# A gather moved behind the bonus products, the first batch's rows turned later, half of the diagonals on ScalarE, and the last rows written in two parts

## The chip, the cores and the metric

The kernel runs on one core of one Trainium2 chip. The metric is the device time of one execution in microseconds (us); lower is better. The profile is one execution taken by the hardware profiler. Its times count from the start of the span. Engines are named as in the profile: PE is TensorE's matmul side and PEld its weight load, DVE is VectorE, ACT is ScalarE, POOL is GpSimd, SP is the engine that issues most DMAs.

## The reference

There are two stages. The first is a linear recurrence with a decaying state for 4 batches, 8 heads, 768 steps and a head dimension of 48:

```python
for t in range(S):
    cur = np.einsum('bhd,bhe->bhde', u[None] * kt, vt)
    y[:, :, t] = np.einsum('bhd,bhde->bhe', rt, state + cur)
    state = w[None, :, :, None] * state + np.einsum('bhd,bhe->bhde', kt, vt)
```

The term with u is the bonus: at its own step a token sees its own k and v weighted by u. The result is laid out as x of 4 batches, 768 tokens and 384 columns. The second stage picks, in each batch, the 128 tokens with the highest score, and only those pass through an MLP:

```python
scores = np.einsum('bsd,d->bs', x, w_gate)
out = x.copy()
for b in range(B):
    top_idx = np.argpartition(-scores[b], capacity)[:capacity]     # capacity = 128
    xe = x[b, top_idx]
    h = np.maximum(xe @ w1, 0.0)                                   # 384 -> 1024
    ye = h @ w2                                                    # 1024 -> 384
    g = 1.0 / (1.0 + np.exp(-scores[b, top_idx]))
    out[b, top_idx] = x[b, top_idx] + g[:, None] * ye
```

## The kernel before

The sequence is cut into units of 128 tokens, six in each batch, 24 in all (NU = 24, NC = 6). Each unit is worked as two halves of 64 tokens. Iteration n of the main loop does a part of unit n - 1, of unit n, of unit n + 1 and of unit n + 2 on different engines. The program order given here is the order in which each engine takes its instructions.

The names: kw is k scaled by powers of the decay; kh and rh are k and r turned by PE and scaled; rp holds the within-unit scores and the state products in PSUM; rk = r * k, rku = rk * u, and du is the sum of rku over each head, the bonus of a token. The matrix at holds du on its diagonal and gets the scores below the diagonal by a masked copy. g and z are states, scr is the product x * w_gate whose sum is the score of a token.

```python
def bonus(n):
    rk = RK[n] = work.tile([128, H, D], F32, name="rk")
    nc.gpsimd.tensor_mul(rk, rpads[n % NIN][:, :, :D], KIN[n])            # line 243
    if n and not picking(n - 1):
        bonus_scaled(n, nc.gpsimd)                                        # rku, line 253

def picking(n):
    return n % NC == 3 and n > NC                                         # n = 9, 15, 21

def diagonal(n):
    AT[n] = work.tile([128, H, C], F32, name="at", bufs=3)
    nc.gpsimd.tensor_mul(AT[n], dia[:, None, :].to_broadcast([128, H, C]),            # line 261
                         DU[n].rearrange("t i p -> t (i p)")[:, :, None].to_broadcast([128, H, C]))
...
for n in range(NU):
    if n == 2:
        late_tables()                  # five small iotas on POOL, lines 222 to 229
    ...
    if n:
        behind = states(n - 1)         # PE line 347, then a mark on ACT (line 351)
    work_at(n, "states")
    products(n)                        # PE line 304
    scores(n)                          # PE line 313
    work_at(n, "scores")
    if picking(n):
        bonus_scaled(n + 1, nc.gpsimd)
    load(n + 4, 0, added(n, 0))        # DVE g, line 328; releases a load of k
    op = masked(n)                     # DVE masked copy, line 318
    load(n + 4, 2, op)
    if n:
        values(n - 1, behind)          # PE line 363, waits for the mark
        finish(n - 1)                  # ACT copies y to x, lines 380 and 382
    if n + 1 < NU:
        pr = turn(n + 1)               # PE lines 270 and 275, ACT kh (line 280)
    if n:
        stored(n - 1)                  # x to DRAM
    if c < NC - 1:
        added(n, 1)                    # DVE g, then ACT z, line 335
    if n + 1 < NU:
        load(n + 4, 1, turned(n + 1, pr))      # DVE rh, line 285
        load(n + 4, 3, bonus_sum(n + 1))       # DVE du, line 257
    if n + 2 < NU:
        scaled(n + 2)                  # POOL kw, line 239
    if n + 1 < NU:
        diagonal(n + 1)                # POOL at, line 261
    if n + 2 < NU:
        bonus(n + 2)                   # POOL rk and rku
    if n:
        weights(n - NC, score(n - 1))  # DVE scr, line 397
    work_at(n, "turn")                 # scores turned along (407, 409), compares (417, 419), ranks, matches (459)
    if n + 1 < NU:
        work_at(n, "end")              # parts of the MLP
```

The second stage is spread over later iterations by a plan. `pick` finds the row numbers idx of the chosen tokens with matmuls (467) and two DVE sums (471, 474). `fetch` gathers these rows from the output in DRAM by an indirect DMA that POOL issues (483). `chosen` turns the rows on PE (499) into xt (ACT, 501). `hidden` and `expert` are the MLP's matmuls (510 and 519), 8 parts each, and `leave` writes the rows back by an indirect DMA (527 and 529):

```python
MOVE0 = (0, 0, 0, 0, 0, 0, 1, 1, 2, 2, 3, 3, 4, 4, 5, 5)
MOVE = (0, 0, 0, 0, 1, 1, 2, 2, 3, 3, 3, 4, 4, 4, 5, 5)

def plan(b):
    n = (b + 1) * NC
    ...
    for z in range(NST):                       # NST = 1
        step(n + 2, "turn", match, b, z)
        step(n + 3, "scores", pick, b, z)
        step(n + 3, "scores", fetch, b, z)
        if b:
            step(n + 5, "scores", chosen, b, z)
        else:
            step(n + 4, "end", chosen, b, z)
    parts = [p for z in range(NST) for p in mlp(b, z)]
    for i, (f, a) in enumerate(parts):
        if b or i >= 2 * NST:
            step(n + 5 + (MOVE if b else MOVE0)[i * 16 // len(parts)], "end", f, *a)
        else:
            step(n + 5, "states", f, *a)
```

After the loop the last batch's tokens are picked, fetched, turned, and their MLP runs alone.

Of the kernel before, what the change touches and what calls it, by code (L numbers as in the profile page):

```python
# [17 lines left out]
def kernel(  # L18
# [23 lines left out]
    nc = tc.nc  # L42
    B, H, S, D = r.shape
    C, T = 64, 128
    NC = S // T
# [16 lines left out]
    work = ctx.enter_context(tc.tile_pool(name="work", bufs=2))  # L62
# [155 lines left out]
    found = const.tile([128, NC], F32)  # L218
    tok = const.tile([128, NU, 5], BF16)

    def late_tables():
        nc.gpsimd.iota(slots, pattern=[[-1, 128]], base=0, channel_multiplier=0,
                       allow_small_or_imprecise_dtypes=True)
        for x in counts:
            nc.gpsimd.iota(x[:, :, 2], pattern=[[-128, NC]], base=-128, channel_multiplier=0,
                           allow_small_or_imprecise_dtypes=True)
        nc.gpsimd.iota(tok[:, :, 0], pattern=[[0, NU]], base=0, channel_multiplier=1,
                       allow_small_or_imprecise_dtypes=True)
        nc.gpsimd.iota(tok[:, :, 1], pattern=[[T, NU]], base=0, channel_multiplier=0,
                       allow_small_or_imprecise_dtypes=True)  # L230
# [10 lines left out]
    def bonus(n):  # L241
        rk = RK[n] = work.tile([128, H, D], F32, name="rk")
        nc.gpsimd.tensor_mul(rk, rpads[n % NIN][:, :, :D], KIN[n])  # L243
        if n and not picking(n - 1):
            bonus_scaled(n, nc.gpsimd)

    def picking(n):

        return n % NC == 3 and n > NC

    def bonus_scaled(n, engine):
        RKU[n] = work.tile([128, H, D], F32, name="rku")
        engine.tensor_mul(RKU[n], RK[n], ub)  # L253
# [4 lines left out]

    def diagonal(n):
        AT[n] = work.tile([128, H, C], F32, name="at", bufs=3)  # L260
        nc.gpsimd.tensor_mul(AT[n], dia[:, None, :].to_broadcast([128, H, C]),  # L261
                             DU[n].rearrange("t i p -> t (i p)")[:, :, None].to_broadcast([128, H, C]))

    def turn(n, keys=None, between=None):
        def two_heads(x, hp):
# [249 lines left out]
    def expert(b, z, f):  # L515
# [5 lines left out]
        if f + 1 == FB:  # L521
            leave(b, z)

    def leave(b, z):
# [4 lines left out]
        st = nc.gpsimd.indirect_dma_start(  # L529
            out=out_rows[: (b + 1) * S, :], out_offset=bass.IndirectOffsetOnAxis(ap=IDX[b, z][:m, :1], axis=0),  # L530
            in_=ot[:m, :], in_offset=None)
# [15 lines left out]
    def step(n, where, f, *a):  # L547
        fill.setdefault((n, where), []).append((f, a))
# [4 lines left out]
        for f in range(FB):  # L553
            yield expert, (b, z, f)


    MOVE0 = (0, 0, 0, 0, 0, 0, 1, 1, 2, 2, 3, 3, 4, 4, 5, 5)
    MOVE = (0, 0, 0, 0, 1, 1, 2, 2, 3, 3, 3, 4, 4, 4, 5, 5)

    def plan(b):  # L560
        n = (b + 1) * NC
        for j in range(NC):
            step(n - NC + j + 2, "turn", scores_along, b, j)
            step(n - NC + j + 2, "turn", compare, b, j)
        step(n + 1, "turn", count, b)
        step(n + 1, "turn", parts_of_scores, b)
        step(n + 2, "turn", rank, b)
        for z in range(NST):
            step(n + 2, "turn", match, b, z)
            step(n + 3, "scores", pick, b, z)  # L570
            step(n + 3, "scores", fetch, b, z)
            if b:
                step(n + 5, "scores", chosen, b, z)
            else:
                step(n + 4, "end", chosen, b, z)
        parts = [p for z in range(NST) for p in mlp(b, z)]
        for i, (f, a) in enumerate(parts):
            if b or i >= 2 * NST:
                step(n + 5 + (MOVE if b else MOVE0)[i * 16 // len(parts)], "end", f, *a)
            else:  # L580
                step(n + 5, "states", f, *a)

    for b in range(B):
        plan(b)
# [1 line left out]
    def work_at(n, where):  # L586
        for f, a in fill.get((n, where), []):
            f(*a)

    bonus(0)  # L590
    warm(10)
    pr = turn(0, k0, key_table)
# [16 lines left out]
    diagonal(0)  # L609
    bonus(1)  # L610
    for n in range(NU):
        if n == 2:
            late_tables()
        b, c = divmod(n, NC)
        if c == 0:
            ZA[n] = zt
        if n:
            behind = states(n - 1)
        work_at(n, "states")
        products(n)  # L620
        scores(n)
        work_at(n, "scores")
        if picking(n):
            bonus_scaled(n + 1, nc.gpsimd)
        load(n + 4, 0, added(n, 0))
        op = masked(n)
        load(n + 4, 2, op)
        if n:
            values(n - 1, behind)
            finish(n - 1)  # L630
        if n + 1 < NU:
            pr = turn(n + 1)
# [50 lines left out]
    for z in range(NST):  # L683
        pick(last, z)
        fetch(last, z)
    some(len(before) - NST)
    for z in range(NST):
        chosen(last, z)
    some(len(before))
    for f, a in after:  # L690
        f(*a)


# [31 lines left out]
```

## Time and profile before

| | before |
|---|---|
| time, median of 3 runs | 164.96 us (164.87 to 165.03) |
| span of the profiled execution | 162.3 us |
| busy PE / PEld | 144.5 / 118.0 us |
| busy DVE / ACT / POOL | 119.6 / 75.9 / 115.2 us |
| mean granted TensorE clock | 0.979 |
| DMA: bytes, mean rate | 24.51 MB, 151 GB/s |
| diagonal (line 261), 24 of them | 28.8 us on POOL, mean 1.20 us |
| score product scr (line 397), 24 of them | 26.3 us on DVE, 0.54 to 4.12 us each |

A line of a timeline has the start, the duration, the engine, the line of the kernel, the operation, the tile written and the tiles read with their shapes, and how many there were; in square brackets stands the idle time before it and what ended that. A line of a table of stretches has the stretch, its length, and then the busy time of PE, PEld, DVE, ACT and POOL with the number of instructions, the granted clock as a share of full speed, the mean busy share of the DMA engines and the rate in GB/s. The chain that ended last is followed back from the last instruction and printed in order of time, with start, duration, engine, tile and line.

### The profile page before, as it was taken

Reading aid. Unit: us, or ns where it says so; the run is one execution under the profiler, and the core shown is the slowest. Engines: PE = TensorE matmul, PEld = TensorE weight load, DVE = VectorE, ACT = ScalarE, POOL = GpSimd, SP = SyncE. Lnnn points to the kernel's source line nnn. Section 1 sums busy time; section 2 is a strip of 40 time slices with the busy share of each in tenths; the row PEclk is TensorE's granted clock in tenths of the full one; section 3 lists DMA queues with packets and bytes.
Section 4 is the critical chain, followed back from the end, with each engine's and each line's share of the span. In section 5 each row is a group of like instructions: output and inputs, shape, how many; then the busy total and the mean of one; then the engine's idle time right before and its main releaser. Section 6 shows DMA issues by size and latency. Waiting matters only on the chain.

```text
span 162.3 us, 8049 instructions
## 1 busy us (share of the span) xinstructions
PE 144.5 (89%) x3374; PEld 118.0 (73%) x3374; DVE 119.6 (74%) x353; ACT 75.9 (47%) x251; POOL 115.2 (71%) x155
## 2 busy tenths in 40 slices
PE   6989978779889948999999999999999999999970
PEld 2577767668777727999786769999877788758730
DVE  7886768889999693358789899999988996701010
ACT  6656565446663631327643747166526565102100
POOL 7389999999999979174798987959999551022002
PEclk9999999999999985799999999999999999999999
DMA  4998999798999986988159989878813104011001
GB/s 74 200 183 155 197 222 208 165 196 188 215 211 223 273 228 163 233 189 220 55 117 253 251 183 206 191 176 181 178 53 101 53 9 146 0 48 49 3 0 48
DMA packets 82660, 24.51 MB, mean 151 GB/s; under 512 B 76352, under 2 KB 82240, under 8 KB 82624
## 3 DMA queue, kind: packets, MB, share of 16 engines
q1 hardware_dynamic: 79888, 19.67, 57.2%
q10 hardware_dynamic: 2224, 2.75, 4.8%
q0 software_dynamic: 512, 1.57, 2.7%
q8 instruction: 27, 0.44, 1.1%
q14 instruction: 9, 0.07, 0.2%
HBM read 18.48 MB, written 5.51 MB: 148 GB/s over the span
## 4 chain that ended last, share of the span: by engine, by line
PE 51%; DVE 18%; issue 11%; POOL 10%; DMA 3%; SPq 2%; ACT 1%; POOLq 1%; DVEq 0%; ACTq 0%
PE m L510 11%; PE rp L304 6%; PE m L519 6%; PE m L270 5%; PE y L347 5%; DVE scr L397 5%; PE rp L313 5%; PE y L363 5%; PE m L275 4%; POOL kw L239 3%; DMA kin<-in_k_dram 2%; DVE oh L459 2%; POOL at L261 2%; DVE at L318 2%; DVE rh L285 2%
## 5 line engine op out<-in xcount | busy, mean ns | idle before, releaser
L261 POOL TENSOR_TENSOR at<-dia,du 128x512 f32<-128x512 f32 x24 | 28.8, 1201 | 14.0 <-DVE du L257 12.6
L397 DVE SCALAR_TENSOR_TENSOR scr<-x,wg 128x384 f32<-128x384 f32 x24 | 26.3, 1094 | 0.4 <-ACT x L382 0.4
L510 PE MATMUL m<-xt,w 128*128 128x128 f32 x192 | 24.6, 286 | 1.7 <-ACT xt L501 1.7
L510 PEld LDWEIGHTS m<-xt,w 128*128 128x128 f32 x192 | 23.5, 201 | 2.4 <-ACT xt L501 2.3
L253 POOL TENSOR_TENSOR rku<-rk,ub 128x384 f32<-128x384 f32 x23 | 23.9, 1040 | 1.6
L239 POOL TENSOR_TENSOR kw<-kin,wk 128x384 f32<-128x384 f32 x23 | 23.3, 1015 | 1.6 <-DMA kin<-in_k_dram 1.6
L335 ACT ACTIVATE z<-g,wp 128x48 f32<-128x48 f32 x80 | 20.2, 325 | 8.6 <-DVE g L328 6.6
L243 POOL TENSOR_TENSOR rk<-rpad,kin 128x384 f32<-128x384 f32 x23 | 23.0, 1001 | 0.0
L380 ACT COPY x<-y 128x192 f32<-128x192 f32 x24 | 7.6, 319 | 32.6 <-PE y L363 30.4
L519 PE MATMUL m<-w,ht 128*128 128x384 f32 x64 | 22.7, 490 | 0.1
L318 DVE COPY_PREDICATED at<-mask,rp 128x512 f32<-128x512 uint32 x24 | 17.6, 732 | 2.7 <-POOL at L261 2.7
L304 PE MATMUL rp<-vpad,kw 128*48 128x96 f32 x288 | 16.7, 257 | 3.0 <-DMA out_dram<-x 1.1
L347 PE MATMUL y<-g,rh 48*64 48x48 f32 x384 | 17.3, 223 | 2.2 <-issue 2.1
L285 DVE TENSOR_TENSOR rh<-m,tables 112x512 f32<-112x512 f32 x24 | 16.4, 683 | 3.0 <-PE m L275 1.6
L347 PEld LDWEIGHTS y<-z,rh 48*64 48x64 f32 x320 | 12.2, 134 | 6.4 <-issue 3.7
L313 PE MATMUL rp<-rh,kh 48*64 48x64 f32 x768 | 16.8, 226 | 0.0
L304 PEld LDWEIGHTS rp<-vpad,kw 128*48 128x48 f32 x288 | 12.7, 127 | 5.2 <-issue 2.3
L419 DVE TENSOR_SCALAR_CACHE_REDUCE gt<-along,sc 128x128 bf16<-128x128 f32 (+5 forms) x24 | 16.2, 675 | 0.0
L257 DVE TENSOR_REDUCE du<-rku 128x8 f32<-128x384 f32 x24 | 13.1, 547 | 3.7 <-POOL rku L253 3.7
L347 PE MATMUL y<-z,rh 48*64 48x48 f32 x320 | 15.4, 223 | 0.5 <-issue 0.5
L270 PE MATMUL m<-ident,kw 128*112 128x128 f32 x92 | 15.0, 285 | 1.0 <-POOL kw L239 0.9
L347 PEld LDWEIGHTS y<-g,rh 48*64 48x64 f32 x384 | 13.8, 134 | 2.8 <-issue 2.6
(99 smaller groups left out, 255.5 us busy)
## 6 DMA issues: line engine op xcount, KB each, us to landing
rpad<-in_r_dram SPq DMA_DIRECT2D x24, 192.0 KB, 4.2
vpad<-in_v_dram SPq DMA_DIRECT2D x48, 96.0 KB, 4.2
kin<-in_k_dram SPq DMA_DIRECT2D x23, 192.0 KB, 4.2
w<-in_moe_w_dram SPq DMA_DIRECT2D x8, 384.0 KB, 4.4
out_dram<-x ACTq DMA_DIRECT2D x14, 192.0 KB, 3.4
out_dram<-x SPq DMA_DIRECT2D x10, 192.0 KB, 3.5
k<-in_k_dram SPq DMA_DIRECT2D x1, 192.0 KB, 2.8
ub<-in_u_dram SPq DMA_DIRECT2D x1, 192.0 KB, 4.3
```

What stands on the lines that cost most here:

```text
L239: (engine or nc.gpsimd).tensor_mul(kws[n % 3][:, :, :D], KIN[n], wk)
L243: nc.gpsimd.tensor_mul(rk, rpads[n % NIN][:, :, :D], KIN[n])
L253: engine.tensor_mul(RKU[n], RK[n], ub)
L261: nc.gpsimd.tensor_mul(AT[n], dia[:, None, :].to_broadcast([128, H, C]), DU[n].rearrange("t i p -> t (i p)")[:, :, None].to_broadcast([128 ...
L270: nc.tensor.transpose(pk[:CH, hp, :], two_heads(kws[n % 3] if keys is None else keys, hp), ident)
L304: nc.tensor.matmul(out=rp[to, hp // 2, at : at + 2 * D], lhsT=kws[n % 3][:, h, :D], rhs=VIN[n][:, h, :], start=True, stop=True)
L313: nc.tensor.matmul(out=rp[ts, i, hp * C : (hp + 1) * C], lhsT=KH[n][rows, hp, ts], rhs=RH[n][rows, hp, ts], start=True, stop=True)
L318: return nc.vector.copy_predicated(at, causal, rp[:, :, : NP * C].rearrange("s i (p t) -> s i p t", p=NP))
L347: mm = nc.tensor.matmul(out=YP[n][i][j * C : (j + 1) * C, hp * D : (hp + 1) * D], lhsT=RH[n][rows, hp, c * C : (c + 1) * C], rhs=z[rows, h ...
L397: return nc.vector.scalar_tensor_tensor(scr, xa[b][:, c, :], 1.0, wg, op0=OP.mult, op1=OP.mult, accum_out=sc[b][:, c : c + 1])
L510: nc.tensor.matmul(out=ph[:, f % 4, :], lhsT=w1[:, d, f * 128 : (f + 1) * 128], rhs=XT[b, z][:, d, :], start=(d == 0), stop=(d == KD - 1))
L519: nc.tensor.matmul(out=pe[:, :Dm], lhsT=HT[b, z][:, f, :], rhs=w2[:, f, :], start=(f == 0), stop=(f == FB - 1))
```

## The change

It has five parts.

- The fetch is issued behind both bonus products on POOL: `pick` and `fetch` move from the place "scores" to a new place "values" (behind the values and before the turning), and rku is always made right behind rk.
- The first batch's rows are turned two iterations after their fetch, as those of the other batches, and its MLP follows the same spread as theirs (MOVE0 goes).
- The iotas move from iteration 2 to the first loads, ahead of the first bonus product.
- In iterations 1 to 10 half of the diagonals (4 of 8 heads) are made by ScalarE as copies with a scale, behind the mark.
- The last batch's second matmul is done in two column halves of 192, each with its own product and its own indirect store of half rows.

The purpose is to take work off POOL where POOL is full, to keep what DVE needs from standing behind the fetch, to keep PE from waiting for the first batch's rows, and to let a half of the last rows leave while PE still works on the other half.

```diff
-    def late_tables():
+    def whole_numbers():
...
         nc.gpsimd.tensor_mul(rk, rpads[n % NIN][:, :, :D], KIN[n])
-        if n and not picking(n - 1):
+        if n:
             bonus_scaled(n, nc.gpsimd)
...
+        du = DU[n].rearrange("t i p -> t (i p)")
+        own = shared(n)
+        nc.gpsimd.tensor_mul(AT[n][:, own:, :], dia[:, None, :].to_broadcast([128, H - own, C]),
+                             du[:, own:, None].to_broadcast([128, H - own, C]))
+
+    def shared(n):
+        return H // 2 if 0 < n < 2 * NC - 1 else 0
+
+    def diagonal_shared(n):
+        du = DU[n].rearrange("t i p -> t (i p)")
+        for h in range(shared(n)):
+            nc.scalar.activation(AT[n][:, h, :], dia, AF.Copy, scale=du[:, h : h + 1])
...
+    def leave_half(b, z, d):
+        m, at = min(128, cap - z * 128), slice(d * Dm // 2, (d + 1) * Dm // 2)
+        ot = work.tile([128, Dm // 2], F32, name="oh", bufs=2 * NST)
+        nc.vector.scalar_tensor_tensor(ot, PE[b, z][:, at], GA[b, z], XR[b, z][:, at], op0=OP.mult, op1=OP.add)
+        nc.gpsimd.memset(spacer, 0.0)
+        st = nc.gpsimd.indirect_dma_start(
+            out=out.rearrange("b s (t d) -> (b s t) d", t=2)[: 2 * (b + 1) * S, :],
+            out_offset=bass.IndirectOffsetOnAxis(ap=HALF[b, z, d][:m, :1], axis=0), in_=ot[:m, :], in_offset=None)
...
-    MOVE0 = (0, 0, 0, 0, 0, 0, 1, 1, 2, 2, 3, 3, 4, 4, 5, 5)
     MOVE = (0, 0, 0, 0, 1, 1, 2, 2, 3, 3, 3, 4, 4, 4, 5, 5)
...
-            step(n + 3, "scores", pick, b, z)
-            step(n + 3, "scores", fetch, b, z)
-            if b:
-                step(n + 5, "scores", chosen, b, z)
-            else:
-                step(n + 4, "end", chosen, b, z)
+            step(n + 3, "values", pick, b, z)
+            step(n + 3, "values", fetch, b, z)
+            step(n + 5, "scores", chosen, b, z)
...
-            if b or i >= 2 * NST:
-                step(n + 5 + (MOVE if b else MOVE0)[i * 16 // len(parts)], "end", f, *a)
-            else:
-                step(n + 5, "states", f, *a)
+            step(n + 5 + MOVE[i * 16 // len(parts)], "end", f, *a)
...
+    whole_numbers()
     bonus(0)
...
-        if n == 2:
-            late_tables()
...
             behind = states(n - 1)
-        work_at(n, "states")
+            diagonal_shared(n)
         products(n)
         scores(n)
         work_at(n, "scores")
-        if picking(n):
-            bonus_scaled(n + 1, nc.gpsimd)
...
             values(n - 1, behind)
             finish(n - 1)
+        work_at(n, "values")
         if n + 1 < NU:
             pr = turn(n + 1)
...
+    for z in range(NST):
+        for d in range(2):
+            at = slice(d * Dm // 2, (d + 1) * Dm // 2)
+            pe = PE[last, z] = psum.tile([128, 512], F32, name="m", bufs=4)
+            for f in range(FB):
+                nc.tensor.matmul(out=pe[:, at], lhsT=HT[last, z][:, f, :], rhs=w2[:, f, at],
+                                 start=(f == 0), stop=(f == FB - 1))
+            leave_half(last, z, d)
```

On POOL the order around the first fetch is, before: rk, fetch, rku, kw, at, rk, rku. After: rk, rku, fetch, kw, at (half), rk, rku.

More of the change, by code (lines that the diff above doesn't have):

```diff
@@ L243, in bonus @@
         nc.gpsimd.tensor_mul(rk, rpads[n % NIN][:, :, :D], KIN[n])
-        if n and not picking(n - 1):
+        if n:
             bonus_scaled(n, nc.gpsimd)
-    def picking(n):
-        return n % NC == 3 and n > NC
     def bonus_scaled(n, engine):
@@ L260, in diagonal @@
         AT[n] = work.tile([128, H, C], F32, name="at", bufs=3)
-        nc.gpsimd.tensor_mul(AT[n], dia[:, None, :].to_broadcast([128, H, C]),
-                             DU[n].rearrange("t i p -> t (i p)")[:, :, None].to_broadcast([128, H, C]))
+        du = DU[n].rearrange("t i p -> t (i p)")
[8 more added lines that the diff above has]
+            nc.scalar.activation(AT[n][:, h, :], dia, AF.Copy, scale=du[:, h : h + 1])
     def turn(n, keys=None, between=None):
@@ L522, in expert, with halves @@
             leave(b, z)
+    def leave_half(b, z, d):
[6 more added lines that the diff above has]
+            out_offset=bass.IndirectOffsetOnAxis(ap=HALF[b, z, d][:m, :1], axis=0), in_=ot[:m, :], in_offset=None)
+        if d:
+            tc.declare_no_dep(st.ins, moves[b, z][-1].ins, reason="the other halves of the rows")
+        left(b, z, st)
+    HALF = {}
+    def halves(b, z):
+        for d in range(2):
+            HALF[b, z, d] = work.tile([128, 1], I32, name=f"half{d}", bufs=NST)
+            with nc.allow_low_precision(reason="whole numbers below 2^24"):
+                nc.vector.tensor_scalar(HALF[b, z, d], IDX[b, z], 2.0, float(d), op0=OP.mult, op1=OP.add)
     def leave(b, z):
@@ L528, in leave, with left @@
         nc.gpsimd.memset(spacer, 0.0)
-        st = nc.gpsimd.indirect_dma_start(
+        left(b, z, nc.gpsimd.indirect_dma_start(
             out=out_rows[: (b + 1) * S, :], out_offset=bass.IndirectOffsetOnAxis(ap=IDX[b, z][:m, :1], axis=0),
-            in_=ot[:m, :], in_offset=None)
+            in_=ot[:m, :], in_offset=None))
+    def left(b, z, st):
         for bb, others in stores.items():
@@ L685 @@
         fetch(last, z)
+        halves(last, z)
     some(len(before) - NST)
@@ L690 @@
     for f, a in after:
-        f(*a)
+        if f is hidden:
+            f(*a)
+    for z in range(NST):
+        for d in range(2):
+            at = slice(d * Dm // 2, (d + 1) * Dm // 2)
[4 more added lines that the diff above has]
+            leave_half(last, z, d)
 _INS = ['r', 'k', 'v', 'w', 'u', 'moe_w_gate', 'moe_w1', 'moe_w2', 'moe_capacity']
```

## The prediction

> **What bounds the kernel now.** I read the busy shares by slice first, then the table of stretches, then each engine's timeline where two engines look full. Times are us from the start of the span. An iteration n (24 of them) is marked by its masked copy on DVE (line 318).
>
> ```profile
> PE 144.5 (89%) x3374; PEld 118.0 (73%) x3374; DVE 119.6 (74%) x353; ACT 75.9 (47%) x251; POOL 115.2 (71%) x155
> ...
> 8.00:20.00 12.00, 10.82 (x329) 9.12 (x329) 8.75 (x22) 7.00 (x22) 11.14 (x11) 1.00 0.92 181
> 20.00:32.00 12.00, 9.34 (x286) 8.06 (x290) 9.63 (x28) 6.90 (x26) 11.80 (x16) 1.00 0.94 197
> 32.00:44.00 12.00, 10.45 (x340) 8.92 (x331) 11.21 (x31) 6.99 (x25) 11.77 (x12) 1.00 0.93 196
> ...
> 56.00:68.00 12.00, 8.84 (x142) 7.55 (x140) 7.26 (x19) 3.38 (x12) 7.77 (x8) 0.72 0.88 206
> 68.00:80.00 12.00, 12.00 (x285) 11.12 (x284) 8.22 (x23) 6.43 (x21) 8.06 (x8) 1.00 0.65 164
> ```
>
> The columns after the length are PE, PEld, DVE, ACT, POOL, then clock, DMA share, GB/s. POOL is full from 8 to about 60 (11.14, 11.80, 11.77 of 12). PE is full from 68 on. Between them lies a hole, 56 to 68, where no engine is full and the clock is 0.72. After 142 comes a tail on one token tile. So there are four stages with four limits.
>
> The hole, on POOL and DVE around the first fetch, and on PE:
>
> ```profile
> 17.23 0.87 DVE L397 SCALAR_TENSOR_TENSOR scr<-x,wg 128x384 f32<-128x384 f32 x1
> ...
> 52.37 1.17 POOL L483 DMA_INDIRECT xr<-out_dram,idx  x1 [0.18 <-DVE at L318]
> 53.58 1.00 POOL L253 TENSOR_TENSOR rku<-rk,ub 128x384 f32<-128x384 f32 x1
> 54.62 0.55 DVE L257 TENSOR_REDUCE du<-rku 128x8 f32<-128x384 f32 x1 [1.22 <-POOL rku L253]
> 55.09 2.81 DVE L397 SCALAR_TENSOR_TENSOR scr<-x,wg 128x384 f32<-128x384 f32 x1
> 56.50 0.99 POOL L243 TENSOR_TENSOR rk<-rpad,kin 128x384 f32<-128x384 f32 x1
> 57.57 1.19 POOL L253 TENSOR_TENSOR rku<-rk,ub 128x384 f32<-128x384 f32 x1
> 61.56 2.93 PE L510 MATMUL m<-xt,w 128*128 128x128 f32 x12 [1.69 <-ACT xt L501]
> ...
> 74.78 1.34 PE m L510 x12
> ```
>
> The second bonus product stands behind the fetch, so the reduction du waits 1.22 for it, and the score product behind du then takes 2.81, where its fastest takes 0.54. PE waits for the chain behind it, and when its first MLP matmuls come it runs at half clock: 2.93 for what takes 1.34 later (last line, from the chain that ended last).
>
> **What the Trainium skill says.** "SBUF — State Buffer", section "Who interferes with whom": a DVE instruction with two SBUF inputs shares a read port with a GpSimd instruction that reads SBUF, one blocks for a whole instruction, and PE and ACT wait for nobody. The trace agrees: scr (x and wg both in SBUF) takes 0.55 beside an idle POOL and 0.87 beside kw, and the diagonal (at) 1.04 alone, 1.36 when scr got in first. The 2.81 is more than one instruction: it ends in the 0.08 gap between rk (ending 57.49) and rku. So a diagonal on ACT costs no port. "TensorE: Matmul & The Clock Gate", section "What's actually happening": the array drops to half clock after an idle window and returns after a busy one. The trace has a granted clock of 0.50 from 60 to 66 after PE had been busy 0.68 of 2 us (56 to 58) and 0.44 of 2 (60 to 62).
>
> **The change part by part.**
>
> *Diagonals.* In n = 1 to 10 POOL writes 128x256 instead of 128x512. From the 0.20 of a 128x6 product and the 1.04 of the diagonal I estimate 0.61, so 0.43 less. POOL's turn (start to start: kw 0.96, at 1.00, rk 1.08, rku 0.96) falls from 4.00 to 3.57, plus 0.32 where scr goes first. ACT gains four activations of 64 columns; four of 48 columns (z) advance it by 0.91, so I take 0.95. Its turn at n = 7 is 2.73 of work (41.51 to 44.24), followed by a wait for y of 1.80 (the other waits are 0.9 to 2.8): the 0.95 goes into that wait, since it stands behind the mark and before x. ACT's sum, 3.68, is below 4.0.
> So what comes next? DVE: from n = 5 to 6 its turn is 4.49 with about 0.25 idle, so 4.2 is its floor; at n = 7 to 8 it idles not at all. And the loads: kin is issued at 16.50, 19.95, 24.54, 27.74, 32.27, 36.59, on average 4.0 apart, 3 to 6 us after its release, with the DMA share at 0.98 to 1.04 in 16 to 28. With the median landing of 4.2, kin for unit 6 is there at 28.7 and its product starts at 30.28; unit 8: 36.5 and 38.91. These slacks of 1.6 to 2.6 cap the gain of this stage.
>
> *Iotas.* They cost POOL 0.63 at 21.00 to 21.63, on a full engine. At 5.9 POOL goes through gone and rk, then waits 1.59 for kin until 8.67: free there.
>
> Together, step by step: masked copy 1 at about 14.4 (before: 14.72), 2 at 18.1 (19.03), 3 at 22.3 (23.98), 4 at 26.6 (28.44), 5 at 31.1 (32.89); from there DVE's own turn repeats. I get 1.8 to 2.3 by n = 8 and book **2.0**.
>
> *Fetch behind both products.* At n = 9 the product rku of unit 10 now comes before the fetch, so du of unit 10 follows rh directly: the 1.22 wait goes. I do not expect scr to be spared: kw, at and rk still follow the fetch without a gap, and scr probably waits for the rk-rku gap again. That gap comes earlier by one rku, and at n = 9 by half a diagonal. du and scr shift by about **1.3**. The same at n = 15 (scr 2.83 at 92.12, on the path: PE waits for it at 95.3) and n = 21 (2.82 at 124.48, PE had other work): I book **0.7** for both. The pick moves behind the values on PE, which end as the masked copy ends, so idx should not stall DVE.
>
> *Rows turned two iterations on.* Before, iteration 11 starts with states, then PE sits 1.69 waiting for xt, then 12 matmuls at half clock (2.93), then products 1.45 and scores 0.96 (0.80 and 0.62 later): scores end at 66.9. After: score product ends 1.3 sooner (56.55 on the old axis), then its two compares, g, masked copy, g, rh take 2.65 as before to 59.2, and scores end at about 59.9 at full clock. Of the 7.0 between 66.9 and 59.9, 1.3 is already booked, and 12 matmuls (1.34) and three transposes (0.48) are only moved to later, where PE is full. Left: 3.9. PE idles about 1.0 in that stretch, as in the iterations before that kept the clock at 1.00; I give 0.9 to the clock staying up and book **3.5**. From 61.56 to 142 PE is busy 79.17 of 80.44, so what is won ahead of that stage reaches the end, and no more than about 1 can be won inside it.
>
> *Last rows in two parts.* Before: 16 expert matmul passes 151.99 to 157.32, product 157.41 (0.62), store issue 158.31 (0.99), then landing. After: 32 passes over 192 columns at half of 0.333, so PE ends where it did (weight loads kept a pace of 0.113 beside line 510). The first half leaves 2.7 earlier and is hidden. The last product is 0.35 (a 128x192 sum) instead of 0.62, and the second store has half the bytes: 0.27 + 0.3 = **0.6**.
>
> Sum: 2.0 + 1.3 + 0.7 + 3.5 + 0.6 = 8.1. From 164.96 this gives 156.9; I say 157.0.
>
> **The rivals.**
> (a) ACT becomes the bound of the first stage: dia, x, kh, z, along and mark are one chain of 3.7, and x, which carried no delay before, now stands behind the diagonals; a late mark delays values. For it: at n = 1 to 3 the wait for y was only 0.85 to 0.91. Against: DVE's 4.2. Then the first stage gives 0.5 to 1 and the total is 158 to 158.5.
> (b) The clock falls anyway, because scr is starved as long and PE waits at the first turning. Then only the 1.69 and about 1 remain of the third part: 159 to 160.
> (c) The loads set the pace from the start (share already 0.92 to 0.99): first stage near 1, total 158.
> (d) The starvation was caused by rku standing behind the fetch; then scr falls to 0.9, all three fetches gain 1.5 to 2 more, total 153 to 155.
> (e) The MLP of the first batch, moved later, crowds iterations 14 and 15 (three parts instead of two), with DVE already at 11.77 of 12 from 92 to 104: gives back up to 1.
>
> **Range and chances.** (a), (b) and (c) together give 161; (d) gives 154. Range 154.0 to 161.0. Faster by over 2% means under 161.66, and the holes at 56 to 68 alone are worth that: 0.88. Within 2%: 0.10. Slower: 0.02, only if the new pick order stalls DVE in every batch or the waits on ACT spread.
>
> **What would show it.** POOL's diagonal near 0.6 and no POOL idle before 40 would prove the first part, with DVE idle gone; POOL waiting for kin would mean (c); masked copies waiting for ACT mean (a). The masked copy of n = 8 at 44.4 (46.45). du right behind rh at n = 9, scr still near 2.5 (under 1 means (d)). Granted clock 1.00 between 50 and 70; anything under 0.9 there means (b). First MLP matmuls 12 in about 1.34. PE busy over 98% after them. The last store issued some 0.3 after the old distance from the last xt. The prediction is wrong if the full PE stage gets longer than its moved 1.8.

## The result and the profile after

The changed kernel takes 160.77 us (median of 4 runs, 159.01 to 161.95), the kernel before 165.0 us beside it on the same chip (164.87 to 165.73). The ratio is 0.970, 95% interval 0.961 to 0.979. Predicted were 157.0 us and a range of 154.0 to 161.0: faster, as said, but the gain is 4.2 us and not 8.0. Single executions of these kernels scatter by some us; the ratios leave disturbed runs out.

Where the time went is read from the masked copies on DVE, one in each iteration (n = 0 to 23). The profiled executions have spans of 162.3 and 158.7 us:

| stretch | before | after | difference | predicted |
|---|---|---|---|---|
| start to copy 1 | 14.72 | 14.39 | -0.3 | -0.3 |
| copy 1 to 8 | 31.73 | 32.32 | +0.6 | -1.7 |
| copy 8 to 11 | 20.80 | 14.50 | -6.3 | -6.6 |
| copy 11 to 23 | 65.30 | 68.44 | +3.1 | +1.1 |
| copy 23 to the end | 29.75 | 29.05 | -0.7 | -0.6 |

"Predicted" sorts the terms of the prediction into the stretches. Copies 8 to 11 get the first fetch (1.3), the rows turned later (3.5) and the 1.8 of matmuls that only move; these 1.8 come back in 11 to 23, less the 0.7 of the other two fetches. Three rows agree within 0.3. Two are wrong by 2.3 and 2.0, and they make up nearly the whole difference to the prediction.

The busy times of the changed kernel, its granted clock, and its table of stretches (columns as before the change: length, PE, PEld, DVE, ACT, POOL, clock, DMA share, GB/s):

```profile
PE 142.5 (90%) x3390; PEld 119.0 (75%) x3390; DVE 118.2 (74%) x356; ACT 86.0 (54%) x291; POOL 112.4 (71%) x157
...
PEclk9999999969999999999999999999999999999998
```

```profile
8.00:20.00 12.00, 11.06 (x331) 9.41 (x333) 9.31 (x22) 9.44 (x34) 11.47 (x12) 1.00 0.89 180
20.00:32.00 12.00, 9.56 (x299) 8.14 (x302) 10.33 (x29) 9.40 (x36) 10.72 (x12) 0.98 0.94 200
32.00:44.00 12.00, 11.20 (x321) 9.70 (x315) 9.51 (x26) 8.37 (x30) 9.46 (x11) 0.88 0.89 188
...
56.00:68.00 12.00, 12.00 (x341) 10.76 (x335) 8.19 (x26) 6.30 (x21) 10.45 (x11) 1.00 0.84 204
```

The hole at 56 to 68 is gone: PE 12.00 of 12 at clock 1.00, where it had 8.84 at 0.72. From 20 to 44, POOL has indeed become idle (10.72 and 9.46, from 11.80 and 11.77), but the stage did not become shorter, and a dip of the clock now lies at 32 to 35, where there was none. So POOL was relieved, and something else set the pace at once.

The chain that ended last names it. It is printed here for 24 to 35 us of the changed kernel (start, duration, what):

```profile
23.80 0.53 PE y L354 x25
24.33 0.57 issue
24.91 0.33 PE y L354 x7
25.23 0.80 PE rp L311 x16
26.03 0.62 PE rp L320 x32
26.66 0.45 PE y L370 x32
27.11 0.58 PE m L277 x4
27.69 0.44 PE m L282 x4
28.12 0.11 PE m L414
28.23 0.61 PE y L354 x29
28.84 1.26 issue
30.11 0.32 PE y L354 x3
...
32.87 1.03 PE m L277 x4
```

Within these 11 us no other engine is in the chain. (Just ahead of it stands a load of r, rpad, from 17.52 to 22.93; PE and POOL each waited 0.6 for it.) PE goes through states, products, scores, values, turning and the scores' turn without a gap: 0.61 + 0.80 + 0.62 + 0.45 + 0.58 + 0.44 + 0.11 = 3.6 us for one iteration. To that comes a stall named "issue", in which PE waits for nothing that the profile shows, in the middle of a run of equal matmuls. Behind the stall of 1.26, with PE idle from 28.84 to 30.11, the granted clock is 0.50 to 0.55 from 32 to 35, and the turning takes 1.03 instead of 0.58. From the scores to the scores' turn the chain takes 3.74 there instead of 2.20, so stall and slow clock together cost 2.8 us.

### The profile page after: what moved, and what is told of

Same layout as the page of the kernel before. It is cut to its first block, busy times and chain, and to the rows that moved or that the text cites. A ratio compares the mean times of both kernels' runs of the same rounds, so it can differ in the third digit from the quotient of the medians.

```text
span 158.7 us, 8130 instructions
## 1 busy us (share of the span) xinstructions
PE 142.5 (90%) x3390; PEld 119.0 (75%) x3390; DVE 118.2 (74%) x356; ACT 86.0 (54%) x291; POOL 112.4 (71%) x157
## 4 chain that ended last, share of the span: by engine, by line
PE 72%; DMA 9%; POOL 6%; issue 6%; SPq 2%; POOLq 1%; DVE 1%; ACT 1%; DVEq 0%; ACTq 0%
PE m L517 14%; PE y L354 8%; PE m L526 8%; PE rp L320 8%; PE rp L311 8%; PE m L277 7%; PE y L370 7%; PE m L282 6%; DMA rpad<-in_r_dram 3%; DMA kin<-in_k_dram 2%; DMA xr<-out_dram,idx 2%; POOL kw L239 2%; DMA out_dram<-x 2%; PE m L720 2%; PE m L414 2%
## 5 line engine op out<-in xcount | busy, mean ns | idle before, releaser
L259 POOL TENSOR_TENSOR at<-dia,du 128x512 f32<-128x512 f32 (+1 forms) x24 | 24.8, 1034 | 11.5 <-DVE du L253 11.4
L239 POOL TENSOR_TENSOR kw<-kin,wk 128x384 f32<-128x384 f32 x23 | 23.9, 1037 | 2.1 <-DMA kin<-in_k_dram 1.8
L404 DVE SCALAR_TENSOR_TENSOR scr<-x,wg 128x384 f32<-128x384 f32 x24 | 24.3, 1013 | 0.4 <-ACT x L389 0.4
L517 PE MATMUL m<-xt,w 128*128 128x128 f32 x192 | 23.5, 277 | 0.3 <-issue 0.3
L517 PEld LDWEIGHTS m<-xt,w 128*128 128x128 f32 x192 | 22.3, 192 | 1.0 <-ACT xt L508 0.5
L354 PE MATMUL y<-g,rh 48*64 48x48 f32 x384 | 16.7, 223 | 1.6 <-issue 1.3
L526 PE MATMUL m<-w,ht 128*128 128x384 f32 x48 | 17.2, 492 | 0.1
L370 PE MATMUL y<-vpad,at 64*64 64x48 f32 x768 | 16.1, 221 | 1.2 <-issue 1.0
L320 PEld LDWEIGHTS rp<-rh,kh 48*64 48x64 f32 x768 | 13.7, 135 | 3.0 <-issue 0.5
L370 PEld LDWEIGHTS y<-vpad,at 64*64 64x64 f32 x768 | 14.1, 138 | 2.0 <-issue 2.0
```

Source lines behind the costliest of these rows:

```text
L239: (engine or nc.gpsimd).tensor_mul(kws[n % 3][:, :, :D], KIN[n], wk)
L259: nc.gpsimd.tensor_mul(AT[n][:, own:, :], dia[:, None, :].to_broadcast([128, H - own, C]), du[:, own:, None].to_broadcast([128, H - own, C]))
L320: nc.tensor.matmul(out=rp[ts, i, hp * C : (hp + 1) * C], lhsT=KH[n][rows, hp, ts], rhs=RH[n][rows, hp, ts], start=True, stop=True)
L354: mm = nc.tensor.matmul(out=YP[n][i][j * C : (j + 1) * C, hp * D : (hp + 1) * D], lhsT=RH[n][rows, hp, c * C : (c + 1) * C], rhs=z[rows, h ...
L370: mm = nc.tensor.matmul(out=YP[n][i][j * C : (j + 1) * C, hp * D : (hp + 1) * D], lhsT=AT[n][ts, i * NP + hp, :], rhs=VIN[n][ts, 2 * hp + ...
L404: return nc.vector.scalar_tensor_tensor(scr, xa[b][:, c, :], 1.0, wg, op0=OP.mult, op1=OP.mult, accum_out=sc[b][:, c : c + 1])
```

## The experiments

All fourteen kernels in one table; the stretches are distances between masked copies in the profiled execution. The time is the median, with the number of runs and, in brackets, the median of the kernel before on the same chip.

| kernel | time, us | 1 to 8 | 8 to 11 | 11 to 15 | 15 to 18 | 18 to 23 | 23 to end |
|---|---|---|---|---|---|---|---|
| before | 165.0 | 31.73 | 20.80 | 22.28 | 17.87 | 25.15 | 29.8 |
| after | 160.77 x4 (165.0) | 32.32 | 14.50 | 23.46 | 18.91 | 26.07 | 29.1 |
| diag_only | 162.57 x4 (165.44) | 30.85 | 18.56 | 23.81 | 19.24 | 26.34 | 29.8 |
| fetch_only | 163.47 x20 (165.44) | 31.78 | 18.02 | 22.41 | 19.30 | 26.49 | 29.8 |
| later_only | 163.96 x4 (165.44) | 31.74 | 16.46 | 23.81 | 18.03 | 26.18 | 29.8 |
| halves_only | 164.23 x20 (165.44) | 31.75 | 19.98 | 22.29 | 16.30 | 26.68 | 29.2 |
| before_light | 164.99 x20 (164.77) | 31.78 | 20.78 | 23.16 | 17.73 | 26.25 | 29.7 |
| after_light | 158.81 x4 (164.77) | 30.22 | 14.71 | 23.10 | 18.08 | 26.32 | 29.0 |
| after_no_diag | 160.58 x4 (164.77) | 31.37 | 14.85 | 22.59 | 18.85 | 26.27 | 29.1 |
| after_gap | 160.55 x4 (164.77) | 30.57 | 14.67 | 23.03 | 20.47 | 26.56 | 29.1 |
| mix | 159.10 x6 (164.25) | 30.47 | 14.00 | 22.63 | 20.07 | 26.52 | 29.1 |
| mix_no_diag | 158.46 x6 (164.25) | 31.11 | 14.83 | 23.66 | 16.28 | 26.68 | 29.1 |
| pe_shift | 162.17 x1 (164.25) | 31.20 | 14.50 | 26.62 | 17.92 | 25.67 | 29.3 |
| after_lighter | 157.12 x1 (164.25) | 29.87 | 13.99 | 22.47 | 18.63 | 25.61 | 29.8 |

One thing is to be seen before any single verdict: the profiled execution of before has the shortest 18 to 23 of all (25.15; the others 25.6 to 26.7). About 1 us of the "+3.1" above is this one execution, not the change. The whole of 11 to 23 scatters too: before, before_light and halves_only have the same program order there and take 65.30, 67.14 and 65.27.

### One part alone: diag_only, fetch_only, later_only, halves_only

The kernel before with the diagonals shared (iotas left where they were), with the fetch moved, with the first batch's rows later, or with the last rows in halves:

```diff
+            diagonal_shared(n)                      # diag_only, with shared(n) = 4 heads in n = 1 to 10
-            step(n + 3, "scores", fetch, b, z)      # fetch_only; pick likewise, rku always behind rk
+            step(n + 3, "values", fetch, b, z)
-                step(n + 4, "end", chosen, b, z)    # later_only, and MOVE for the first batch
+            step(n + 5, "scores", chosen, b, z)
+            leave_half(last, z, d)                  # halves_only
```

> The kernel before with the shared diagonals alone. Theory (the loads set the pace of the first 45 us, POOL only looked like the bound): the masked copy of n = 8 stays within 0.6 us of 46.45, POOL shows idle before the diagonal or before kw, and the time is 164.3 to 165.3. Rival (POOL was the bound and ACT takes the work for nothing): that copy comes 1.5 to 2 us earlier and the time is 163 to 163.5. Second rival (ACT's longer turn costs): it comes later and the time is 166.

> The kernel before with pick and fetch moved behind the values and rku always right behind rk. Theory: du no longer waits at n = 9, but the score product behind the fetch still takes over 2.5 us at n = 15 and 21, because nothing opens a gap on POOL; at n = 15 POOL now stands before the fetch until the pick is done. Gain 0.5 to 1.5: 163.5 to 164.5. Rival (the place of rku caused the long score product): all three fall under 1.4 us and the time is 161.5 to 163.

> The kernel before with the first batch's rows turned two iterations on and its MLP spread as the others'. Theory (most of the gain of the whole change comes from here): the wait of PE for xt and the half clock from 60 to 66 go, masked copy of n = 13 comes 3 to 4 us earlier than 78.50, time 161.2 to 162.5. Rival (the clock falls without this part too, since PE still idles behind the starved score product): only 1 to 1.7 is won, 163.3 to 164.

> The kernel before with only the last batch's second matmul and store in two column halves. Both theories: PE of this part stays 5.3 to 5.4 us, the last store is half as long, gain 0.5 to 0.8, time 164.2 to 164.5. Rival: the second store queues behind the first, gain under 0.2.

Measured against before: diag_only 0.985 (0.978 to 0.991), fetch_only 0.997 (0.990 to 1.003), halves_only 0.989 (0.985 to 0.992); later_only scattered too much for a ratio. These ratios are hints only: before itself ran from 161.82 to 169.58 us in its 39 runs there, and before_light below has 1.012 (1.007 to 1.016) although its median is 0.2 us from that of before. The stretches say more.

- diag_only: 1 to 8 falls by 0.9, less than the rival's 1.5 to 2. (Copy 8 comes at 46.06, within the theory's 0.6 of 46.45, but copy 1 comes 0.5 later here, so that sign decides nothing.) A larger gain lies in 8 to 11 (20.80 to 18.56), where the score product at n = 9 took 0.55 instead of 2.81 although nothing about the fetch was changed. In this execution both are lost again from 11 to 23 (69.39 against 65.30).
- fetch_only: 8 to 11 falls by 2.8, with scr at 0.55 at n = 9. At n = 15 it stays at 2.98, and 15 to 18 is 1.4 longer. Its ratio is not distinguishable from 1.
- later_only: 8 to 11 falls by 4.3, although its granted clock still drops to 0.50 in 52 to 56 and 0.73 in 56 to 60. Here too scr took 0.55 at n = 9. Copy 13 comes at 75.24, 3.3 earlier, as the theory said.
- halves_only: the end of the kernel is shorter by 0.6 in the trace. The ratio would be worth 1.8 us, which has no place in the parts that the change touches; the medians are 1.2 apart, and its quickest run (162.21) is not below that of before (161.82). So the 0.6 rests on the trace alone.

So the long scr at n = 9 (2.8 us) is hit or miss: it came in before, before_light and halves_only, and not in diag_only, fetch_only, later_only. It is no fixed price of the old order of instructions. With the fetch behind both products it did not come at n = 9 at all: in the nine kernels with that order there (fetch_only, the changed kernel and those made from it) scr took 0.55 to 1.33 there.

### What sets the first stage: before_light, after_light, after_no_diag

To see whether the loads hold the first stage, r and v of units 6 to 11 are loaded for 4 of the 8 heads only, in the kernel before and in the changed one; the values of the other heads are left out. after_no_diag is the changed kernel with all diagonals on POOL.

```diff
+        if part and NC <= n < 2 * NC:               # before_light, after_light
+            to, x = to[:, : H // 2, :], x[: H // 2]
-        return H // 2 if 0 < n < 2 * NC - 1 else 0  # after_no_diag
+        return 0
```

> The kernel before with the same lighter loads of units 6 to 11 (output not the reference's). Theory: POOL sets the pace there, so masked copies 1 to 8 stay 31.7 us apart (31.73 before) and the time changes by less than 0.7 in this stage. Rival (the loads were the bound already): the distance falls by over 1.

> The kernel after with r and v of units 6 to 11 loaded for four of the eight heads only (the other heads keep old data, so the output of these units is not the reference's); the number of loads is the same, their bytes fall from 576 to 384 KB a unit. Theory (with half the diagonals gone from POOL the DMA traffic sets the pace, through late loads and late instruction blocks of PE): masked copies 1 to 8 lie 28.5 to 30 us apart instead of 32.3, POOL does not wait for kin or rpad, PE has fewer waits named issue, time 2 to 3.5 under the kernel after. Rival (ACT's longer turn or the order of PE sets the pace): the distance stays at 31 to 32.5.

> The kernel after with all diagonals on POOL again. Theory: POOL is the bound again, masked copies 1 to 8 lie 31.1 apart (31.73 less the 0.63 of the iotas, which stay moved), the time is within 1 of the kernel after, in either direction. Rival (the shared diagonals are worth what was predicted): 1.5 to 2.5 slower than the kernel after.

Every kernel with all diagonals on POOL and the iotas in iteration 2 takes 31.73 to 31.78 from copy 1 to 8, with the light loads too: POOL sets the pace there, and the loads add nothing. Moving the iotas alone gives 31.37 and 31.11 (after_no_diag, mix_no_diag). With the diagonals halved on top (full loads: after, after_gap, mix, pe_shift) it is 32.32, 30.57, 30.47, 31.20, on average 31.14. Over the whole stretch the diagonals moved to ScalarE thus bring nothing that can be told from the scatter, and after_no_diag has the time of the changed kernel (160.58 against 160.77). Split at copy 2, the stretch shows more. From copy 1 to 2 the seven kernels with halved diagonals take 3.67 to 3.78, the seven with all diagonals on POOL 4.31 to 4.34: the 0.6 is won there, in every kernel. From copy 2 to 8, with the iotas moved and full loads, it is 26.79 to 28.54 with halved diagonals and 26.78 and 27.03 without: after the first step nothing more is won.

The lighter loads decide little. after_light takes 30.22, between what its theory (28.5 to 30) and its rival (31 to 32.5) said, and its stalls did not become fewer (4.2 us from 10 to 60 us, 3.8 in the changed kernel). Against the best kernels with full loads (30.47, 30.57) it is shorter by 0.3, so the loads are at most a small part.

It was not the cost of the shared diagonals. The shared diagonals in the changed kernel, from its groups kept apart by shape, POOL first, then ACT:

```profile
L259 POOL TENSOR_TENSOR at<-dia,du 128x256 f32<-128x256 f32 x10 | 8.3, 828 | 2.9 <-DVE du L253 2.9
```

```profile
L269 ACT ACTIVATE at<-dia,du 128x64 f32<-128x64 f32 x40 | 10.6, 336 | 1.2 <-DVE du L253 1.0
```

POOL's half takes 0.83 on average: 0.61 where scr doesn't hold it up (50.02 in the timeline), 0.93 where scr went first (21.44). ACT's four parts advance it by 1.06. Both are near the estimates (0.61 alone, 0.32 more behind scr; 0.95), and ACT's chain is not what ends last between 24 and 35.

### Whose stalls these are: pe_shift, after_lighter

In the changed kernel the stalls split the states' 32 matmuls into 25 and 7 at n = 3 and into 29 and 3 at n = 4; at n = 6 the products' 16 into 6 and 10. pe_shift puts 16 one-column matmuls (32 PE instructions) at the very start, beside the first loads. after_lighter loads r and v of units 6 to 11 for 1 of 8 heads only (the others' values are left out).

```diff
+    few = psum.tile([128, 512], F32, name="m", bufs=4)        # pe_shift
+    for _ in range(16):
+        nc.tensor.matmul(out=few[:, :1], lhsT=busy[:, :128], rhs=busy[:, :1], start=True, stop=True)
```

```diff
+        if part and NC <= n < 2 * NC:                         # after_lighter
+            to, x = to[:, :1, :], x[:1]
```

> The changed kernel with 16 more one-column matmuls (32 more TensorE instructions, about 1 us beside the first loads) at the start. Theory (the stalls named issue come where TensorE's own instructions arrive in pieces of equal length): they move 16 matmuls ahead in the kernel's own stream: the one of n=3, which splits the states' 32 matmuls into 25 and 7, then splits them into about 9 and 23, and that of n=4 from 29 and 3 to about 13 and 19; their sum over 10 to 60 us stays. Rival (they are a wait for data or for a buffer that the trace doesn't name): they stay ahead of the same matmuls as in the changed kernel, 25 and 7, 29 and 3.

> The changed kernel, loading r and v of units 6 to 11 for 1 of 8 heads only (the output is not the reference's). Theory (the loads' traffic lengthens TensorE's stalls): 1 to 8 falls from 30.2 (with half the heads) or 32.3 to 28.5 to 29.5, and the waits named issue ahead of matmuls fall by half. Rival (traffic has nothing to do with them): 1 to 8 stays at 30 to 31 and the waits as they are.

The chain of pe_shift at the same two iterations:

```profile
23.41 0.48 PE y L354 x9
23.89 0.27 issue
24.15 0.56 PE y L354 x23
...
28.02 0.43 PE y L354 x12
28.46 0.23 issue
28.69 0.55 PE y L354 x18
```

The stalls moved with the instruction stream: 9 and 23 where there had been 25 and 7, and 14 (2 + 12) and 18 where there had been 29 and 3, so 16 and 15 matmuls earlier. They belong to places in PE's own stream of instructions and not to the data of these matmuls. The spacing fits: from one stall to the next lie the 121 matmuls of an iteration and 4 to 5 more, some 251 instructions (each matmul has its weight load), and the DMA queues in the page of the changed kernel have this line (packets, MB, share):

```profile
q8 instruction: 27, 0.44, 1.1%
```

2 x 3390 PE instructions in 27 packets are 251 each. That these packets are PE's instructions is concluded from this agreement; the trace does not name the engine that they are for. What makes a stall long is open; mix_no_diag has 1.0 us of them within 10 to 60 us, mix 3.3. The expected constant sum failed: PE's stalls within 10 to 60 us add up to 6.5 in pe_shift and 3.8 in the changed kernel. And after_lighter contradicts the theory that the loads' traffic is the cause: 3.5 us of stalls, not half of 3.8, and 29.87 from copy 1 to 8, between what theory and rival said.

### The fetch behind both products: after_gap, mix, mix_no_diag

after_gap puts a small memset on POOL between the products behind the fetch, to leave scr a gap. mix is the changed kernel with only the first fetch behind both products and the others where they were before; mix_no_diag is mix with all diagonals on POOL.

```diff
+            nc.gpsimd.memset(gapmark, 0.0)                            # after_gap
-            step(n + 3, "values", fetch, b, z)                        # mix; pick likewise
+            step(n + 3, "scores" if b else "values", fetch, b, z)
+    def picking(n):
+        return n % NC == 3 and n > 2 * NC
```

> The kernel after with a memset of one element on POOL between kw and the diagonal in each iteration, which reads nothing from SBUF. Theory (scr is starved because POOL's reading products follow each other without a gap behind an indirect DMA): scr behind the fetches of n = 15 and 21 falls from 2.87 to under 1.0, masked copies 15 to 16 from 7.5 to about 5.7, time 1 to 2 under the kernel after. Rival (descriptor work of the indirect DMA itself holds the port): scr stays over 2.5 there.

> The changed kernel, but only the first fetch (n=9) stands behind both bonus products; those of n=15 and n=21 and their products stand where the kernel before has them. Theory (the fetch behind both products helps at n=9 alone and costs about 1 us at n=15, where GpSimd now reaches the fetch before the pick is there): masked copies 15 to 18 take 17.9 to 18.2 us instead of 18.9, 8 to 11 stays at 14.5 to 14.9, and the time is about 159.8, 1.0 below the changed kernel. Rival (what n=15 loses is lost again behind the fetch, since the products then wait for it): 15 to 18 stays at 18.8 to 19.3 and the time at 160.5 to 161.

> The kernel of mix, with all diagonals on GpSimd. Theory (the diagonals on ScalarE bring only what TensorE's own chain leaves over, 0.5 us or less): masked copies 1 to 8 take 31.4 us, and the time is within 1 us of mix. Rival (GpSimd's diagonals are worth the 0.5 us of each iteration that was predicted): 1 to 8 at 31.4 against 30 or less in mix, and the time 1.5 us or more above mix.

after_gap: scr takes 0.57, 0.55 and 3.25 behind the three fetches of the loop (the changed kernel 1.33, 2.87 and 3.24), and the time stays at 160.55. Of these, only the 0.55 at n = 15 speaks for the gap: the six kernels with the same order there and no gap have 2.87 to 3.08, while at n = 9 scr was short without a gap too, and at n = 21 it stayed long. What a short scr is worth does not show: copies 15 to 16 were to fall to 5.7 and take 8.63, since a stall of 1.79 and half clock behind it lie in the same iteration. So the 1.5 to 2 us that rival (d) gave to it is neither shown nor refuted.

mix was to bring 15 to 18 down to 18; it has 20.07 (its time is 159.10, 159.8 expected, with single runs from 154.97 to 162.41). But mix_no_diag, which has the same order there, has 16.28. The difference is a stall again, in the table of stretches of mix:

```profile
82.00:84.00 2.00, 0.53 (x23) 0.47 (x22) 1.36 (x5) 0.20 (x1) 1.44 (x2) 1.00 0.47 96
84.00:86.00 2.00, 2.00 (x34) 1.91 (x27) 0.00 (x0) 1.45 (x5) 1.54 (x2) 0.56 1.09 318
86.00:88.00 2.00, 2.00 (x7) 1.26 (x6) 1.62 (x4) 1.14 (x6) 0.35 (x1) 0.59 1.13 214
```

PE waited 1.47 within the values ("issue") and was busy for 0.53 of the 2 us from 82 to 84, and then ran at a clock of 0.56 to 0.59 for 4 us, about 2 us lost. So this experiment does not decide where the later fetches should stand: 15 to 18 scatters from 16.3 to 20.5 over the kernels, more than the 1 us in question.

What mix and mix_no_diag do show is a change of the bound in the first stage. The summary of the chain between 14 and 46 us, first mix (half of the diagonals on ACT), then mix_no_diag (all on POOL), in both of which the line numbers from rku on are four higher than in the changed kernel:

```profile
by line: PE rp L315 20.4%; PE y L358 16.4%; PE rp L324 13.7%; PE m L281 12.7%; issue 10.6%; PE y L374 9.9%; PE m L286 8.2%; ACT at L273 3.3%; PE m L418 2.0%; ACT x L393 2.0%; DVE du L257 1.8%; ACT x L391 0.1%
```

```profile
by line: POOL at L263 28.7%; POOL rk L243 18.1%; POOL kw L239 15.3%; POOL rku L253 13.8%; DMA kin<-in_k_dram 13.6%; issue 11.0%; DVE at L329 2.3%; DVE g L339 0.6%; POOLq L239 0.2%
```

With all diagonals on POOL the chain of this pair is POOL's (76%), with PE absent. With half of them on ACT it is PE's (83%), with POOL absent. From copy 1 to 8 this is 30.47 against 31.11; the gain of 0.6 is that of copy 1 to 2 (3.68 against 4.33), from 2 to 8 they are equal (26.79 and 26.78). In time mix_no_diag is not behind mix (158.46 against 159.10). The ratio of mix_no_diag to before is 0.969 (0.962 to 0.976), that of the changed kernel 0.970 (0.961 to 0.979): no version here is shown to beat the changed kernel.

## Why the prediction held only near its upper end

That 160.77 lies inside the range is partly luck. The upper end of 161 stood for rivals (a), (b) and (c) together, and none of the three came as described; the loss came from elsewhere.

*Diagonals and iotas (2.0 booked): the term that failed.* The durations and the relief of POOL were right, and so were the first two steps: copies 1 and 2 came at 14.39 and 18.17 (14.4 and 18.1 predicted), but copies 3, 4 and 5 at 22.84, 27.76 and 32.37 (22.3, 26.6 and 31.1). The step that failed is "So what comes next? DVE: ... 4.2 is its floor"; the cap by the loads was not reached. Next came PE, whose own iteration is 3.6 and which stalls once in an iteration, for 0.1 to 1.3 us. In mix its states start at 19.91 and, five iterations on, at 42.53, 4.52 apart on average, no shorter than the 4.32 at which POOL's diagonals follow one another in mix_no_diag (22.66, 26.98, 31.30 in the chain). PE's chain can be added up from the timeline of before (the prediction itself used several of its terms). The chain that ended last in before even runs over PE from 23.00 to 38.52 (but for one store), through a stall of 1.20, and over DVE only from there:

```profile
28.54 0.76 PE y L347 x28
29.30 1.20 issue
30.50 0.32 PE y L347 x4
```

POOL did not wait for that stall: its kw start at 25.95, 30.28 and 34.60, 4.3 apart as elsewhere. So PE was level with POOL already, and the prediction, which read "POOL is full" as the bound, did not add PE up. In the changed kernel copy 8 came at 46.71 instead of 44.4. Without a dip of the clock in this stage copy 1 to 8 takes 30.47 (mix), 30.57 (after_gap) and, with the longest stalls, 31.20 (pe_shift), which wins 0.5 to 1.3 where 1.7 was booked; with the dip, nothing. Rival (a), ACT, did not happen: in mix's chain from 14 to 46 ACT has 5%. Nor does any load stand in that chain, as rival (c) would have it.

*Fetch at n = 9 (1.3) and rows turned later (3.5): right.* Copy 8 to 11 fell by 6.3 instead of 6.6, and all eight kernels with both parts take 13.99 to 14.85 there. The two pieces of evidence named for it are there: the clock is 1.00 from 44 to 128 us, and the first matmuls of the MLP run at full speed, as the chain of the changed kernel shows:

```profile
62.98 2.68 PE m L517 x24
...
69.27 1.34 PE m L517 x12
```

24 in 2.68 are twice the 1.34 for 12, where the kernel before had paid 2.93 for 12. The wait of 1.69 for xt has gone. "Scr still near 2.5" was wrong: it took 1.33, and 0.55 to 0.86 in the other kernels with this order at n = 9, which is what rival (d) said, for this fetch alone. That the sum still agrees is partly luck: PE also lost 1.75 ahead of 50.20 (put down to a store of x) and a stall of 1.13 ahead of 55.15, and neither was booked. How the 6.3 divides between the two parts is open. Alone they show 4.3 (rows) and 2.8 (fetch), but both with scr at 0.55, and diag_only, which has neither part, shows 2.2 with scr at 0.55.

*Fetches at n = 15 and 21 (0.7): not shown.* The sentence "idx should not stall DVE" failed at n = 15 of the changed kernel. The timelines of DVE and of POOL in the changed kernel:

```profile
86.25 0.16 DVE L478 TENSOR_REDUCE idx<-m 128x1 int32<-128x2 f32 x1 [0.87 <-PE m L474]
...
88.24 2.87 DVE L404 SCALAR_TENSOR_TENSOR scr<-x,wg 128x384 f32<-128x384 f32 x1
```

```profile
86.69 1.03 POOL L490 DMA_INDIRECT xr<-out_dram,idx  x1 [2.39 <-DVE picked L481]
```

A stall of 0.97 held up the values on PE, so the pick behind them came late; DVE waited 0.87 for it and POOL, which has nothing but the fetch to do by then, 2.39 (before: 0.81). after_no_diag and after_gap have the same wait on POOL (1.62 and 3.03), behind stalls of 0.83 and 1.79 within the values too; in fetch_only the stall there was 0.63, DVE did not wait for idx, and POOL waited 0.60. scr was not spared either. At n = 21 it was even longer in the seven kernels with the new place of the fetch (3.21 to 3.25) than in the seven without (2.78 to 2.82). 15 to 16 takes 7.51 against 6.48 before. By the table, 15 to 18 is no better in fetch_only than in before; mix left open how much of this is the order and how much the stalls.

*The full stage "no longer than its moved 1.8": wrong by 2.* Rival (e) does not show: 11 to 15, where the moved matmuls run, grew by 1.2. Of +3.1 instead of +1.1, about 1 is the order at n = 15 with its stall (15 to 18: +1.0 instead of a gain), and 0.9 is the short 18 to 23 in the profiled execution of before. The sign that PE is busy over 98% failed too: from the first MLP matmuls to the last fetch (62.98 to 139.30) it is busy for 73.70 of 76.32, idle for 2.6 where it was 1.3 before. Since 11 to 23 scatters by nearly 2 between kernels of one order, how much of the 2 belongs to the change stays open.

*Last rows in halves (0.6): right.* 0.7 in the changed kernel, 0.6 alone. The end of its chain, with the first of the two halves:

```profile
149.26 2.62 PE m L720 x16
...
151.96 0.43 DVE oh L535
```

The product of a half took 0.43, and the last one, at 154.50, 0.42 (estimated 0.35, before 0.62). "The first half leaves 2.7 earlier" holds nearly: the two stores are issued at 152.66 and 155.20, 2.5 apart. From the last xt to the last store it is 12.10, and 12.31 before: 0.2 less, as the sum has it, and not "0.3 after the old distance". The rest is the shorter end behind that issue.

## What to carry to other kernels

When an engine is relieved, add up the serial chain of every other engine for one iteration, with its stalls, and not only its busy share: here PE at 78 to 90% busy from 8 to 44 us in the kernel before had 3.6 us of work and one stall in an iteration, together no less than POOL's 4.3, and so of 1.7 us booked at most 1.3 came, 0.4 to 0.6 of it from the iotas. Read the chain that ended last beside the busy shares: from 23 to 38 us it named PE here before the change. A hole in which no engine is full was the safer place for a large change: the 6.3 us won there are near the 6.6 computed. Where a transfer's index comes from a chain over two engines, moving it behind more work lets every delay of that work through to the engine that issues it.

## What was not expected of the hardware

- PE stalls at places fixed in its own instruction stream, about every 251 instructions, for 0.1 to 1.9 us; 32 instructions more at the start moved two of these places by 16 and 15 matmuls. Lighter loads did not remove them.
- Stalls of 1.26 us (changed kernel) and 1.47 us (mix) were each followed by 3 to 4 us at half clock. The Trainium skill, "TensorE: Matmul & The Clock Gate", section "What's actually happening", names a free-running window of about 3.4 us of activity. From the granted clock in slices of 1 us (0.75, 0.50, 0.50, 0.55 from 31 to 35, changed kernel; 0.61, 0.50, 0.50, 0.68 from 84 to 88, mix; 0.75 is a slice with half of it at half clock) both drops last about 3.4 us, which agrees with that length. But an idle time of less than half of it was enough to bring one on, with PE busy 0.84 of 2 us (28 to 30, changed kernel) and 0.53 of 2 (82 to 84, mix); idle times of 0.57, 0.80 and even 1.75 (ahead of 50.20, changed kernel) and 1.86 (pe_shift) were followed by no drop. So the length of one idle time does not tell; no run here separates what does.
- The score product behind an indirect DMA takes either 0.55 or 2.8 to 4.1 us with the same order of instructions (at n = 15 2.83 in before and 0.55 in before_light). The Trainium skill, "SBUF — State Buffer", section "Who interferes with whom", has the instruction that was issued first hold the shared port pair for its whole length while the other waits; POOL's products take 1.0 to 1.36 here, so 2.8 is more than one of them. A gap on POOL brought it to 0.55 at n = 15, and did not at n = 21.
